# Attention scores of two head groups issued in turns from the lower and the upper 64 partitions, into two PSUM banks

## The chip, the cores and the metric

The kernel runs on one core of a Trainium2 chip. The metric is device time in microseconds (us) of one execution. Three runs of the kernel before took 887.04, 887.59 and 899.56 us (median 887.59). One more execution was profiled; all rows in this text come from it.

## The reference, cut to what matters

Attention over 4 batches, 8 heads, 768 positions and 64 dimensions per head, with a mask (8 global keys and the last 96 local ones) and a bias per head, then two mixture-of-experts layers on its output.

```python
scores = scale * np.matmul(q, k.transpose(0, 1, 3, 2))
scores = scores + bias[None, :, :, :]
scores = np.where(keep, scores, -1000000000.0)
scores = scores - np.max(scores, axis=-1, keepdims=True)
a = np.exp(scores)
a = a / (np.sum(a, axis=-1, keepdims=True) + 1e-09)
attn = np.matmul(a, v)
# x: attn as 3072 rows of 512; then twice, each with 8 experts and the expert of the largest logit:
#   out[row] = gate[row] * (relu(x[row] @ w1[e]) @ w2[e])
```

## The kernel before

**Tiling of the attention.** The 3072 query rows are 24 units of 128 (a batch has six, `QT = 6`). A unit has 8 heads in four groups of two, `HEADS = [(0, 2), (1, 3), (4, 6), (5, 7)]` (L237). Query and key are transposed so that two heads lie one above the other: even heads in partitions 0 to 63, odd heads in 64 to 127. So groups 0 and 2 read the lower half and groups 1 and 3 the upper half (`p0`, L592). A query sees at most 232 keys: 128 of its own block and 104 others (the first unit of a batch: 128 alone).

**The stages of one group g of unit u**, each a function that issues its instructions when called:

- `score` (S, L589): every product is three matmuls (high by high, high by low, low by high part), contracted over 64 partitions. Two heads times two pieces of keys (128 and 104 columns) times three is 12 matmuls, each with a weight load of its own, into one PSUM bank `sp` of the pool tag "A". The first unit of a batch has 6.
- `rowmax` (R, L608), one per head: VectorE (DVE) adds the bias, writes `e` to SBUF and the negative row maximum `nm`. It is the only reader of `sp`; after both, the bank is free.
- `expo` (X, L620): ScalarE (ACT) takes the exponential. `etrans` (T, L625): TensorE (PE) transposes `e`, fp32, four pieces, into a bank `et` of tag "B".
- `e_hi` (EH, L636) on ACT and `e_lo` (EL, L642) on DVE split `et` into a high and a low part, `eh` and `el`.
- `pv` (PV, L648): 12 matmuls with the values, into `xp` of tag "D".

Beside the groups, a unit transposes its keys and queries (`tp`, L555) and its output row (`xtp`, L692), computes the logits (`lp`, L417) and its place in the expert's list (`pr`, L460 to L462), with small work on DVE (L425 to L471, L668 to L702) and splits of query, key and value on GpSimd (POOL).

**What sets the order.** Each tag has two PSUM banks (`bufs=2`, eight banks in all); a third `bank("A", ...)` waits until the first is read out. Nothing is scheduled by a compiler: a `Timeline` sorts all calls by a number, `4 * u + g + OFF[name]`, and calls them in that order (L1095 to L1118); each engine then works strictly in its own order. `OFF` has "S" 0.1, "R0" 0.6, "R1" 0.8, "X0" 1.3, "X1" 1.8, "T0" and "T1" 2.2, "EH" 3.1, "EL" 3.5, "PV" 4.3. So on PE a group's scores stand ahead of the transposes of two groups earlier and of the values' products of four groups earlier, and so on group by group.

**After the attention** the experts' work is one long run of matmuls (L870, L889), whose weights arrive during the attention's last units and are split on ACT and DVE.

Of the kernel before, what the change touches and what calls it, by code (L numbers as in the profile page):

```python
# [12 lines left out]
BF16 = mybir.dt.bfloat16  # L13
# [7 lines left out]
B, H, S, D = 4, 8, 768, 64  # L21
# [23 lines left out]
OFF = {  # L45
# [5 lines left out]
}  # L51
ENG = {
    "kh": "P", "vh": "P", "qh": "P", "mh": "P", "ml": "P", "pp": "P", "pf": "V", "po": "V", "wa": "V",
# [47 lines left out]
def kernel(  # L101
# [3 lines left out]
    nc = tc.nc  # L105
# [20 lines left out]
    def bank(tag, name):  # L126
        return psum.tile([128, 512], F32, tag=tag, name=name)
# [24 lines left out]
    def load(u, nm):  # L152
        b, t = divmod(u, QT)
        q0 = t * 128
        d = st.setdefault(u, {})
        d[nm] = ld.tile([128, H, D], F32, tag=f"ld_{nm}", name=f"ld_{nm}", bufs=4 if nm == "v" else 3)
        nc.sync.dma_start(out=d[nm], in_={"q": q, "k": k, "v": v}[nm][b, :, q0:q0 + 128, :].rearrange("h p d -> p h d"))
# [79 lines left out]
    HEADS = [(0, 2), (1, 3), (4, 6), (5, 7)]  # L237
# [184 lines left out]
    def pick_m(d, lg, row):  # L422

        d["lg"] = lg
        nc.vector.max(out=best_of(row), in_=lg)  # L425

    def pick_i(d, row):
        d["ix"] = small.tile([128, 8], U32, tag="ix", name="ix")
        nc.vector.max_index(out=d["ix"], in_max=best_of(row), in_values=d["lg"])

    def pick_f(d, eng=nc.vector):
        d["ixf"] = small.tile([128, 1], F32, tag="ixf", name="ixf")
        eng.tensor_copy(out=d["ixf"], in_=d["ix"][:, 0:1])

    def pick_o(d, valid, eng=nc.vector):

        oh = d["oh"] = small.tile([128, E], BF16, tag="oh", name="oh")
        if valid is None:
            eng.tensor_scalar(out=oh, in0=iota8, scalar1=d["ixf"], scalar2=None, op0=ALU.is_equal)
        else:  # L440
            nc.vector.tensor_scalar(out=oh, in0=iota8, scalar1=d["ixf"], scalar2=valid, op0=ALU.is_equal, op1=ALU.mult)
# [15 lines left out]
    def place_m(m, d):  # L457

        d["pr"] = bank("C", "pr")[:, 0:E]
        nc.tensor.matmul(out=d["pr"], lhsT=ones_b[0:1, :], rhs=rowoff_b, start=True, stop=False)  # L460
        nc.tensor.matmul(out=d["pr"], lhsT=ones_b, rhs=acc[m], start=False, stop=False)
        nc.tensor.matmul(out=d["pr"], lhsT=before, rhs=d["oh"], start=False, stop=True)  # L462

    def place_t(m, d):
        t2 = small.tile([128, E], F32, tag="t2", name="t2")
        d["pos"] = small.tile([128, 1], F32, tag="pos", name="pos")
        nc.vector.scalar_tensor_tensor(out=t2, in0=d["pr"], scalar=1.0, in1=d["oh"], op0=ALU.mult, op1=ALU.mult,
                                       accum_out=d["pos"])

    def place_a(m, d, eng=nc.vector):  # L470
        eng.tensor_tensor(out=acc[m], in0=acc[m], in1=d["oh"], op=ALU.add)  # L471
# [73 lines left out]
    def t_in(u, nm):  # L545

        d = st[u]
        if nm == "q":
            d["qt"] = aw.tile([128, 2, 4, 128], F16, tag="qt", name="qt", bufs=3)
        else:  # L550
            d["kt"] = kt_of[u] = aw.tile([128, 2, 4, 128 + GMAX], F16, tag="kt", name="kt", bufs=3)
        tp = d["tp", nm] = bank("C", "tp").rearrange("p (i c) -> p i c", i=4)
        src = d[nm].rearrange("p (i e) d -> p i (e d)", e=2)
        for i in range(4):
            nc.tensor.transpose(tp[:, i, :], src[:, i, :], ident)  # L555

    def t_out(u, nm):
        d = st[u]
        f = d["f", nm] = aw.tile([128, 4, 128], F32, tag=f"f{nm}", name=f"f{nm}")
        nc.scalar.activation(out=f, in_=d["tp", nm], func=ACTF.Copy, scale=-0.125 if nm == "q" else 1.0)  # L560
# [27 lines left out]

    def score(u, g):  # L589

        d = st[u]
        p0 = 64 * (HEADS[g][0] % 2)  # L592
        sp = d["sp", g] = bank("A", "sp").rearrange("p (j c) -> p j c", j=2)
        keys = [(slice(WB - 128, WB), d["kt"], 0)]
        if u % QT:
            keys.append((slice(0, NA), kt_of[u - 1], 128 - LMAX + 1))
        else:
            keys[0] = (slice(0, 128), d["kt"], 0)
        for j, h in enumerate(HEADS[g]):
            for cols, kt, c0 in keys:  # L600
                for n, (x, y) in enumerate(((0, 0), (0, 1), (1, 0))):
                    lq = d["qt"][p0:p0 + 64, x, h // 2, :]
                    rk = kt[p0:p0 + 64, y, h // 2, c0:c0 + cols.stop - cols.start]
                    nc.tensor.matmul(out=sp[:, j, cols], lhsT=lq.bitcast(BF16) if x else lq,  # L604
                                     rhs=rk.bitcast(BF16) if y else rk, start=(n == 0), stop=(n == 2),
                                     skip_group_check=True)

    def rowmax(u, g, j):  # L608

# [476 lines left out]
    def off_of(u, nm):  # L1086

        w = (u - NU + 3) / 2 if nm in LAST and u > NU - 3 else 0
        return w * LAST.get(nm, 0) + (1 - w) * OFF[nm]

    def eng_of(nm):
        return nc.gpsimd if ENG[nm] == "P" else nc.vector


    tl = Timeline()  # L1095
    for u in range(NU):
        n = 4 * u
        for nm in "v" if u == 0 else "kqv":
            tl.at(SOFF.get(f"ld{nm}{u}", n + OFF["ld" + nm]), lambda u=u, nm=nm: load(u, nm))
        for nm, fn in (("tq", lambda u: t_in(u, "q")), ("tk", lambda u: t_in(u, "k")),  # L1100
                       ("fq", lambda u: t_out(u, "q")), ("fk", lambda u: t_out(u, "k")),
                       ("qh", q_hi), ("ql", q_lo), ("kh", k_hi), ("kl", k_lo), ("vh", v_hi), ("vl", v_lo),
                       ("rt", route_t), ("rh", route_h), ("rl", route_lo),
                       ("lg", route_l), ("pm", lambda u: pick_m(st[u], st[u]["lp"], st[u]["row"])),
                       ("pi", lambda u: pick_i(st[u], st[u]["row"])), ("pf", lambda u: pick_f(st[u], eng_of("pf"))),
                       ("po", lambda u: pick_o(st[u], None, eng_of("po"))),
                       ("wm", lambda u: place_m(0, st[u])), ("wt", lambda u: place_t(0, st[u])),
                       ("wa", lambda u: place_a(0, st[u], eng_of("wa"))), ("place", route_p)):
            tl.at(SOFF.get(f"{nm}{u}", n + off_of(u, nm)), lambda u=u, fn=fn: fn(u))
        for g in range(4):  # L1110
            for nm, fn in (("S", score), ("EH", e_hi), ("EL", e_lo), ("PV", pv)):
                tl.at(n + g + OFF[nm], lambda u=u, g=g, fn=fn: fn(u, g))
            for nm, fn in (("R", rowmax), ("X", expo), ("T", etrans)):
                for j in range(2):
                    tl.at(n + g + OFF[f"{nm}{j}"], lambda u=u, g=g, j=j, fn=fn: fn(u, g, j))
        for i in range(2):
            for nm, fn in (("fs", fin_s), ("fr", fin_r), ("fx", fin_x)):
                tl.at(n + 2 * i + 1 + off_of(u, nm), lambda u=u, i=i, fn=fn: fn(u, i))  # L1118
# [28 lines left out]
    _, left = slots(tl, 1, t0, t0 + MOFF["table1"])  # L1147
# [30 lines left out]
```

## Time and profile before

| | |
|---|---|
| Three runs | 887.04, 887.59, 899.56 us |
| The profiled execution | 892.53 us (span of its instructions 891.0 us) |
| Attention's scores | from 10.2 to 224.1 us of the span |
| Experts' matmuls end the kernel | the chain that ended last is PE from 634 us on |

The profile names engines PE (matmuls), PEld (weight loads), DVE, ACT, POOL and SP. A busy share is not a measure of what bounds: an engine that is full in a stretch, and has no wait in it, is. Durations of matmuls include their way through the array, so successive matmuls overlap in the list; the pace is read from the starts. "L604" is line 604 of the kernel.

### The profile page before, as it was taken

What the parts mean: (1) busy time and instruction counts of PE and PEld (TensorE: products, weight loads), DVE (VectorE), ACT (ScalarE), POOL (GpSimd) and SP (SyncE); (2) the same over time, 40 slices, a digit from 0 to 9 for tenths busy, and PEclk for the clock granted to TensorE, in tenths of its full rate; (3) what the DMA queues carried; (4) which work ended last, traced back from release to release, by engine and by line L of the source; (5) the groups of instructions that cost most, each with busy time, mean ns of one, the idle gap of its engine ahead of it and who ended that gap; (6) DMA issues with size and microseconds to landing.
All of it is one profiled execution on the core that took longest, in us unless ns stands there. A gap on an engine that the chain in (4) does not pass through costs nothing. (4 is left out here: it accounts for less than half of the span.)

```text
span 891.0 us, 30257 instructions
## 1 busy us (share of the span) xinstructions
PE 830.5 (93%) x10153; PEld 632.3 (71%) x10153; DVE 476.9 (54%) x1745; ACT 401.9 (45%) x858; POOL 305.9 (34%) x495
## 2 busy tenths in 40 slices
PE   5999999999688999999999788969999999999995
PEld 4888888888566777677777566647677777777773
DVE  5668898899843747656573634646311125111133
ACT  5568888888513434525341524332222225222242
POOL 6358777785432333423341422102111111111110
PEclk9999999999699999999999899999999999999998
DMA  8657766677249989987887684832562117322200
GB/s 145 177 150 211 181 147 144 155 193 226 66 104 267 248 185 240 221 262 181 248 240 168 148 216 135 213 116 52 150 162 69 52 50 209 78 62 52 51 28 16
DMA packets 227582, 133.99 MB, mean 150 GB/s; under 512 B 177148, under 2 KB 199676, under 8 KB 227360
## 3 DMA queue, kind: packets, MB, share of 16 engines
q1 hardware_dynamic: 220896, 112.10, 51.5%
q0 software_dynamic: 6320, 19.37, 6.2%
q8 instruction: 85, 1.39, 0.7%
q14 instruction: 137, 1.12, 0.4%
q10 hardware_dynamic: 144, 0.00, 0.0%
HBM read 79.54 MB, written 33.77 MB: 127 GB/s over the span
## 5 line engine op out<-in xcount | busy, mean ns | idle before, releaser
L870 PE MATMUL hp<-mx,h 128*128 128x128 f16 x3520 | 326.4, 222 | 9.6 <-ACTq L896 7.7
L870 PE MATMUL hp<-mx,l 128*128 128x128 f16 x1760 | 312.8, 222 | 7.0 <-DVEq L896 3.9
L870 PEld LDWEIGHTS <-h 128*128 128x128 f16 x3520 | 278.9, 99 | 48.7 <-ACTq L896 10.6
L881 DVE SCALAR_TENSOR_TENSOR hl<-hp,hh 128x256 bf16<-128x256 f32 x220 | 93.1, 423 | 268.7 <-ACT hh L880 139.4
L880 ACT ACTIVATE hh<-hp 128x256 f16<-128x256 f32 x220 | 84.2, 383 | 272.0 <-PE hp L870 233.8
L870 PEld LDWEIGHTS <-l 128*128 128x128 bf16 x1760 | 174.6, 99 | 8.8 <-DVEq L896 4.6
L889 PE MATMUL y<-l,hh 128*128 128x512 bf16 x440 | 167.5, 381 | 1.4 <-DVEq L896 1.4
L889 PE MATMUL y<-h,hh 128*128 128x512 f16 x440 | 167.7, 381 | 0.0
L889 PE MATMUL y<-h,hl 128*128 128x512 f16 x440 | 167.3, 380 | 0.0
L347 DVE TENSOR_TENSOR l<-st,h 128x1024 bf16<-128x1024 f32 x88 | 111.9, 1273 | 52.3 <-ACTq L896 25.3
L889 PEld LDWEIGHTS <-hh 128*128 128x128 f16 x880 | 77.4, 98 | 53.3 <-issue 0.8
L120 ACT CAST h<-st 128x1024 f16<-128x1024 f32 x88 | 91.2, 1043 | 50.7 <-SPq L909 20.7
L934 POOL DMA_INDIRECT out_dram<-o,ti x26 | 27.0, 1040 | 227.3 <-ACTq L896 189.9
L479 POOL DMA_INDIRECT xs<-r,posi x29 | 33.3, 1150 | 176.2 <-DVEq L896 61.3
L623 ACT ACTIVATE e<-e,nm 128x232 f32<-128x232 f32 (+1 forms) x192 | 84.0, 470 | 7.3 <-DVE nm L616 5.1
L889 PEld LDWEIGHTS <-hl 128*128 128x128 bf16 x440 | 43.2, 98 | 54.1 <-issue 2.2
L604 PE MATMUL sp<-kt,qt 64*128 64x128 f16 (+3 forms) x1056 | 77.8, 225 | 2.5 <-DVE nm L616 1.9
L604 PEld LDWEIGHTS <-qt 64*128 64x128 f16 (+1 forms) x1056 | 61.8, 101 | 14.5 <-issue 11.1
L616 DVE CUSTOM_DVE_ANT_0 e<-sp,bias_mid 128x232 f32<-128x232 f32 x160 | 61.3, 385 | 5.7 <-PE sp L604 5.6
L646 DVE TENSOR_TENSOR el<-et,eh 128x512 bf16<-128x512 f32 (+1 forms) x96 | 60.9, 634 | 1.7 <-ACT eh L640 1.7
L640 ACT CAST eh<-et 128x512 f16<-128x512 f32 (+1 forms) x96 | 52.4, 546 | 19.0 <-PE et L634 17.3
L634 PE MATMUL et<-ident,e 128*128 128x128 f32 x192 | 50.7, 297 | 1.0 <-ACT e L623 1.0
(201 smaller groups left out, 1138.9 us busy)
## 6 DMA issues: line engine op xcount, KB each, us to landing
st<-in_moe_w_dram SPq DMA_DIRECT2D x88, 512.0 KB
mxf<-xs SPq DMA_DIRECT2D x29, 266.0 KB
x_d<-r SPq DMA_DIRECT2D x29, 256.0 KB
ld_k<-in_k_dram SPq DMA_DIRECT2D x24, 256.0 KB
ld_q<-in_q_dram SPq DMA_DIRECT2D x24, 256.0 KB
ld_v<-in_v_dram SPq DMA_DIRECT2D x24, 256.0 KB
row<-xg SPq DMA_DIRECT2D x24, 256.0 KB
xs<-empty SPq DMA_DIRECT2D x18, 266.0 KB
```

The lines of the kernel that those rows point to most:

```text
L120: nc.scalar.copy(out=out, in_=in_)
L347: (nc.vector if engines[i][1] == "V" else nc.gpsimd).tensor_tensor(out=l, in0=w, in1=h, op=ALU.subtract)
L604: nc.tensor.matmul(out=sp[:, j, cols], lhsT=lq.bitcast(BF16) if x else lq, rhs=rk.bitcast(BF16) if y else rk, start=(n == 0), stop=(n == 2 ...
L616: nc.vector.tensor_tensor_reduce(out=d["e", g][:, j, 0:w], in0=d["sp", g][:, j, 0:w], in1=(bias_mid if t else bias_first)[:, HEADS[g][j], ...
L623: nc.scalar.activation(out=e, in_=e, func=ACTF.Exp, bias=d["nm", g][:, j:j + 1], scale=-1.0)
L634: nc.tensor.transpose(tp[:, j, :], e[:, j, NA if t else 0:WB if t else 128], ident)
L640: nc.scalar.copy(out=eh[:, 0:n], in_=d["et", g][:, 0:n])
L646: nc.vector.tensor_tensor(out=el[:, 0:n], in0=d["et", g][:, 0:n], in1=d["eh", g][:, 0:n], op=ALU.subtract)
L870: nc.tensor.matmul(out=hp[:, j, :], lhsT=w[p][:, c, fs], rhs=r.bitcast(BF16) if x else r, start=(n == 0), stop=(n == 11))
L880: nc.scalar.activation(out=hh, in_=hp, func=ACTF.Relu)
L881: nc.vector.scalar_tensor_tensor(out=hl, in0=hp, scalar=0.0, in1=hh, op0=ALU.max, op1=ALU.subtract)
L889: nc.tensor.matmul(out=d["y"], lhsT=d[hx, p][:, j, :], rhs=w[p][:, j, :], start=(p == 0 and j == 0 and i == 0), stop=(p == NP - 1 and j == ...
```

## The change

`score` now serves two groups at a time: it takes both banks of tag "A" and issues the matmuls of groups g and g+1 in turns, one from partitions 0 to 63 into the one bank, one from 64 to 127 into the other. Number, shapes and operands of the matmuls and weight loads stay. It is called for even g only, at the even group's number. For the odd group, R is called 0.6 earlier and X 0.3 earlier (`oddR`, `oddX`); T, EH, EL and PV keep their numbers.

```diff
-    "c0s": 1.3, "c1": 15.6, "c1s": 2.0, "rl": 10.6,
+    "c0s": 1.3, "c1": 15.6, "c1s": 2.0, "rl": 10.6, "oddR": 0.6, "oddX": 0.3, "oddT": 0.0,
...
     def score(u, g):
...
-        d = st[u]
-        p0 = 64 * (HEADS[g][0] % 2)
-        sp = d["sp", g] = bank("A", "sp").rearrange("p (j c) -> p j c", j=2)
+        d = st[u]
+        sp = [bank("A", "sp").rearrange("p (j c) -> p j c", j=2) for _ in range(2)]
+        for i in range(2):
+            d["sp", g + i] = sp[i]
...
-        for j, h in enumerate(HEADS[g]):
+        for j in range(2):
             for cols, kt, c0 in keys:
                 for n, (x, y) in enumerate(((0, 0), (0, 1), (1, 0))):
-                    lq = d["qt"][p0:p0 + 64, x, h // 2, :]
...
+                    for i in range(2):
+                        h = HEADS[g + i][j]
+                        p0 = 64 * (h % 2)
+                        lq = d["qt"][p0:p0 + 64, x, h // 2, :]
+                        rk = kt[p0:p0 + 64, y, h // 2, c0:c0 + cols.stop - cols.start]
+                        nc.tensor.matmul(out=sp[i][:, j, cols], lhsT=lq.bitcast(BF16) if x else lq,
+                                         rhs=rk.bitcast(BF16) if y else rk, start=(n == 0), stop=(n == 2),
+                                         skip_group_check=True)
...
         for g in range(4):
-            for nm, fn in (("S", score), ("EH", e_hi), ("EL", e_lo), ("PV", pv)):
+            if g % 2 == 0:
+                tl.at(n + g + OFF["S"], lambda u=u, g=g: score(u, g))
+            for nm, fn in (("EH", e_hi), ("EL", e_lo), ("PV", pv)):
...
             for nm, fn in (("R", rowmax), ("X", expo), ("T", etrans)):
                 for j in range(2):
-                    tl.at(n + g + OFF[f"{nm}{j}"], lambda u=u, g=g, j=j, fn=fn: fn(u, g, j))
+                    t = n + g + OFF[f"{nm}{j}"] - (OFF[f"odd{nm}"] if g % 2 else 0)
+                    tl.at(t, lambda u=u, g=g, j=j, fn=fn: fn(u, g, j))
```

On PE, in a unit in the middle of the attention, the third group's scores start behind the transposes of an output row. Before, the matmuls that follow go to one bank, `sp_3470`:

```order
L692 MATMUL xtp_3460<-ident_97,row_3318 128x128 x4
L604 LDWEIGHTS qt_3121
L604 MATMUL sp_3470<-kt_3039,qt_3121 128x128
L604 LDWEIGHTS qt_3121
L604 MATMUL sp_3470<-kt_3039,qt_3121 128x128
```

In the changed kernel the same place has two banks in turns, `sp_3471` and `sp_3472`, 24 matmuls in all, and the fourth group's place has none:

```order
L697 MATMUL xtp_3460<-ident_97,row_3322 128x128 x4
L609 LDWEIGHTS qt_3122
L609 MATMUL sp_3471<-kt_3053,qt_3122 128x128
L609 LDWEIGHTS qt_3122
L609 MATMUL sp_3472<-kt_3053,qt_3122 128x128
L609 LDWEIGHTS qt_3122
```

So PE has, from one pair's scores to the next, two sets of transposes and two of values' products, where each group's scores stood between them before.

On DVE, in a unit's first two groups, the row maxima (`e,nm<-sp` with `nm` behind it) of one group stood apart from those of the next, with the output's product `row` and a split `el` between them. Before:

```order
L646 TENSOR_TENSOR el<-et,eh 128x512
L616 ISA e,nm<-sp,bias_mid 128x232
L616 ISA nm 128x1
L433 CAST ixf<-ix 128x1
L672 RECIPROCAL rs<-rs 128x4
L616 ISA e,nm<-sp,bias_mid 128x232
L616 ISA nm 128x1
L682 TENSOR_TENSOR row<-xp,rs 128x256
L646 TENSOR_TENSOR el<-et,eh 128x512
L616 ISA e,nm<-sp,bias_mid 128x232
L616 ISA nm 128x1
```

In the changed kernel:

```order
L651 TENSOR_TENSOR el<-et,eh 128x512
L621 ISA e,nm<-sp,bias_mid 128x232
L433 CAST ixf<-ix 128x1
L677 RECIPROCAL rs<-rs 128x4
L621 ISA e,nm<-sp,bias_mid 128x232
...
L621 ISA e,nm<-sp,bias_mid 128x232
...
L621 ISA e,nm<-sp,bias_mid 128x232
L621 ISA nm 128x1
L687 TENSOR_TENSOR row<-xp,rs 128x256
L651 TENSOR_TENSOR el<-et,eh 128x512
```

All four row maxima of the pair now stand together, and `row`, both splits and the small work stand behind the fourth.

## Rows read from the trace of the kernel before

**Rows 1.** The page: span, and its 40 slices of PE, DVE and PEclk.

```profile
span 891.0 us, 30257 instructions
...
PE   5999999999688999999999788969999999999995
...
DVE  5668898899843747656573634646311125111133
...
PEclk9999999999699999999999899999999999999998
```

**Rows 2.** Busy us (and instructions) per engine, seven stretches of one unit each.

```profile
core 0: us, PE busy (x) PEld busy (x) DVE busy (x) ACT busy (x) POOL busy (x), PEclk, DMA share, GB/s
92.88:101.50 8.62, 8.62 (x142) 7.63 (x140) 7.91 (x37) 7.39 (x17) 6.81 (x11) 1.00 0.73 181
...
sum 60.35, PE 60.35 PEld 53.51 DVE 54.66 ACT 51.86 POOL 46.62; mean PE 8.62 PEld 7.64 DVE 7.81 ACT 7.41 POOL 6.66
```

**Rows 3.** PE in order of time, a late unit: start us, us, line, operands, count.

```profile
200.66 0.17 PE L417 MATMUL lp<-wgl,rxh 128*128 128x8 bf16 x1
200.69 0.17 PE L417 MATMUL lp<-wgh,rxl 128*128 128x8 f16 x1
...
211.67 0.19 PE L661 MATMUL xp<-vs,el 128*128 128x65 f16 x1
211.79 0.78 PE L604 MATMUL sp<-kt,qt 64*128 64x128 f16 x12
212.50 0.33 PE L633 MATMUL et<-ident,e 128*128 128x128 f32 x1
...
213.00 0.23 PE L661 MATMUL xp<-va,eh 104*128 104x65 f16 x2
...
213.37 0.63 PE L692 MATMUL xtp<-ident,row 128*128 128x128 f32 x4
213.93 0.78 PE L604 MATMUL sp<-kt,qt 64*128 64x128 f16 x12
```

**Rows 4.** PE in order of time, between 22 and 55 us.

```profile
22.28 1.31 PE L604 MATMUL sp<-kt,qt 64*128 64x128 f16 x12 [1.17 <-DVE nm L616]
...
34.54 1.34 PE L604 MATMUL sp<-kt,qt 64*128 64x128 f16 x12
...
49.32 0.24 PE L661 MATMUL xp<-vs,el 128*128 128x65 f16 x1
49.49 1.34 PE L604 MATMUL sp<-kt,qt 64*128 64x128 f16 x12
50.76 0.47 PE L633 MATMUL et<-ident,e 128*128 128x128 f32 x1
...
54.55 0.33 PE L633 MATMUL et<-ident,e 128*128 128x128 f32 x1
```

**Rows 5.** Busy us per engine, the attention from 54.5 us on and the stretch behind.

```profile
54.50:224.10 169.60, 166.33 (x2639) 145.94 (x2636) 151.72 (x708) 139.63 (x307) 126.14 (x189) 1.00 0.69 178
224.10:245.00 20.90, 12.35 (x164) 10.82 (x162) 18.00 (x50) 12.37 (x20) 9.54 (x13) 0.67 0.21 53
```

**Rows 6.** What PE waited for from 54.5 to 224 us, the largest: us, times, longest.

```profile
PE pr L460 <- DVE rxl L702: 2.3, 4, 0.8
```

**Rows 7.** Groups of instructions, 54.5 to 224 us: busy us, mean ns of one, idle before.

```profile
L623 ACT ACTIVATE e<-e,nm 128x232 f32<-128x232 f32 (+1 forms) x161 | 70.5, 472 | 2.7 <-DVE lead_f L502 1.3 <-DVE nm L616 0.6 <-DVE rs L672 0.5
L604 PE MATMUL sp<-kt,qt 64*128 64x128 f16 (+1 forms) x901 | 60.2, 213 | 0.0
L616 DVE CUSTOM_DVE_ANT_0 e<-sp,bias_mid 128x232 f32<-128x232 f32 x137 | 52.5, 384 | 0.0
L646 DVE TENSOR_TENSOR el<-et,eh 128x512 bf16<-128x512 f32 (+1 forms) x80 | 51.1, 638 | 0.0
L604 PEld LDWEIGHTS <-qt 64*128 64x128 f16 x899 | 47.3, 94 | 8.1 <-issue 6.5
L640 ACT CAST eh<-et 128x512 f16<-128x512 f32 (+1 forms) x81 | 44.5, 550 | 8.8 <-PE et L634 7.2 <-PE xp L661 0.6
```

More of the change, by code (lines that the diff above doesn't have):

```diff
@@ L598, in score @@
             keys[0] = (slice(0, 128), d["kt"], 0)
-        for j, h in enumerate(HEADS[g]):
+        for j in range(2):
             for cols, kt, c0 in keys:
                 for n, (x, y) in enumerate(((0, 0), (0, 1), (1, 0))):
-                    lq = d["qt"][p0:p0 + 64, x, h // 2, :]
[L603 to L606, printed above, removed]
+                    for i in range(2):
[6 more added lines that the diff above has]
+                                         skip_group_check=True)
     def rowmax(u, g, j):
```

## The prediction

> **What bounds the kernel now.** I read the page first: PE is full in nearly every slice, DVE is at 80 to 90% up to the eleventh and well below later [rows 1]. The change touches the attention alone, so it is priced there and carried to the end: behind it PE runs the experts' matmuls almost without a stop, so time won before 224 us should reach the end. Next come the stretches of one unit. They all take 8.62 to 8.63 us; PE fills every one, DVE is busy 7.81 us in the mean, ACT 7.41, POOL 6.66 [rows 2]. From 54.5 to 224.1 us PE is busy 166.33 of 169.60 us [rows 5], and the largest of its few waits, 2.3 us, is for something that the change leaves alone [rows 6]. So in this stretch PE is the bound, with DVE only 0.8 us per unit behind: that 0.8 us, and not what PE saves, is the ceiling of the gain.
>
> Before 54 us it is another regime. The same twelve scores that take 0.71 us from their first start to the next instruction at 211.79 take 1.27 us at 49.49, and the transpose behind them takes 0.47 us in place of 0.33 [rows 3, 4]. TensorE is at the lower of its two levels (1.2 GHz) until some point between 51 and 54.5 us and at 2.4 GHz after, although the page's clock line shows 9 from the first slice [rows 1]; the durations decide. A unit there takes 14.95 us (34.54 to 49.49) [rows 4], far above DVE's 7.8, so PE bounds it with room.
>
> **What a block of scores costs.** At 2.4 GHz: 0.71 us from the first score to the transpose behind it, and ahead of it 0.12 us from the last values' matmul, where such matmuls follow each other at about 0.03 (twelve from 213.00 to 213.37) [rows 3], so 0.09 us of entry. That is 0.80 us, four times a unit, 3.2 of 8.62. The twelve matmuls have (128+104)/2 = 116 columns in the mean, 48 ns at 2.4 GHz, some 0.6 us for twelve; the other 0.2 us is spent on the way in and out of a block.
>
> **The change, part by part.**
>
> *Fewer blocks.* Two blocks of 24 in place of four of 12 save two entries and exits: 2 x 0.2 = about 0.4 us a unit. This part needs no overlap of matmuls.
>
> *Turns between halves.* If a matmul from the lower half runs beside one from the upper half, 24 take the time of 12. No row shows two such matmuls side by side: the halves never met without transposes between them in the stretch read. Bounds: no overlap saves nothing more, PE needs 8.62 - 0.4 = 8.2 us a unit; full overlap makes the pair's block 0.80 us, PE needs 8.62 - 1.6 = 7.0 us. Against overlap stands the issue: every matmul has a weight load. The logits' matmuls, 8 columns each with a weight load of its own, start 25 to 30 ns apart [rows 3], so two loads and two matmuls can be issued in some 52 to 60 ns, about the 48 ns of one stream; issue hardly takes it away. I take full overlap.
>
> The Trainium skill (TensorE: Matmul & The Clock Gate, Measured speedup vs the span model) says that matmuls in different row groups run side by side, each further one costing about 4 ns; by it the pair's block would be 0.85 us by estimate and PE's unit 7.1 us. The same page says that a weight load overlaps a running matmul only when the row groups differ. The trace differs there: loads of 94 ns [rows 7] hide behind matmuls of the same rows, at some 52 ns from one to the next [rows 3], so no gain of that kind is left.
>
> *Who is next.* With PE at 7.0, DVE at 7.81 sets the unit, and ACT at 7.41 is close. PE today reaches 98% of its stretch (166.33 of 169.60) with the runner-up at 90% [rows 5]. DVE would have one runner-up at 95% and stand in a chain with it, so I give it 96%: 7.81 / 0.96 = 8.1 us. Bounds: 7.81 (never idle) and 8.62 (as now).
>
> *The added wait.* A pair needs both "A" banks, so its second matmul waits for the fourth row maximum of the pair before, and transposes and values' products of the older groups queue behind it on PE. The wait's length: four row maxima at 384 ns [rows 7], 1.54 us, and small work between them. PE has 2.3 us of other work behind the scores in the shorter of the two gaps: two sets of transposes at 0.50, two of values' products at 0.37, one row transpose at 0.56 [rows 3]. So PE stands still little there. On the other side DVE has, behind the fourth maximum, two splits of 638 ns [rows 7], 1.28 us, and `row` and small work on top, while the next pair's block takes 0.8 and its last matmul another 0.21 to arrive [rows 7]. DVE stays fed; I cost it at nothing beyond the 96%. If that cover were gone, each pair would cost 1.0 us of DVE, 2.0 a unit. DMA, busy 0.69 of this stretch [rows 5], would rise to 0.74 with the shorter units and stays hidden.
>
> *ACT's new order.* Three exponentials in a row ahead of the odd group's split: 3 x 472 + 550 = 2.0 us [rows 7], then the split on DVE, 0.64, ahead of the next pair's maxima. With the first maximum that is some 3.3 us around, under half a unit at 8.1. No cost.
>
> **Sum.** From 54.5 to 224.1 us: 169.6 x (1 - 8.1/8.62) = 10.2 us. At the bounds: 16 with DVE full; 8 for fewer blocks alone with PE still full; 0 if nothing is won.
>
> From 24.5 to 54.5 us at 1.2 GHz: a block costs 1.27 + 0.11 of entry (49.32 to 49.49 less 0.06, twice the 0.03 above) = 1.38 [rows 4]; two fewer per unit leave 14.95 - 2.76 = 12.2 us. Thirty us hold 2.0 units now and 2.46 then; 0.45 units at the later price of 8.1 are 3.6 us, if the clock rises when it does now. Before 24.5 PE waits for row maxima (1.17 us at 22.28 [rows 4]); I count 0 there, within 1.5 us either way. Behind 224.1 DVE is busy 18.0 of 20.9 us [rows 5] with work that the change leaves alone: 0, up to 2 lost.
>
> Together 13.8 us. The profiled execution took 892.5 us, so its like would take 878.7; it lay 4.9 us over the median of the three runs, 887.6. Against that median: **873.8, say 874 us**.
>
> **The rivals.**
>
> *The clock rises earlier.* PE is dense from 24.5 us on, yet only behind 51 did the clock rise. With half the blocks there are fewer breaks in PE's stream. Every us by which it rises earlier is worth 1 - 8.1/12.2 = 0.34 us; 15 us earlier gives 5 more: 869 us, and 20 us 867. For it: the stream gets denser. Against: nothing in the rows says what made it rise.
>
> *No overlap.* PE needs 8.2 us a unit and stays the bound: 169.6 x 0.4/8.62 = 8 us less at most, and about 0.9 from the slow part (two entries and exits of some 0.2 a unit, two units): 879; with PE held now and then by the two banks, 882.
>
> *The two banks hold PE.* If row maxima come late in each pair, transposes behind the scores come late too, then exponentials' splits, then DVE: a round that closes on itself. At half of the 1.0 us per pair, the unit is 8.1 + 1.0 = 9.1, and 169.6 us become 179: 9.4 - 3.6 = 6 us slower, 893. Against: the cover above, 1.28 us and more against 1.0.
>
> *Slower: the clock stays low.* With DVE the bound, PE stands still a tenth of the time; the clock did fall in the stretch behind the attention (mean 0.67, PE busy 12.35 of 20.9 us [rows 5]). A unit at 1.2 GHz would take 12.2 in place of 8.1, 4.1 us more; from eight units on (a third of the attention) it loses more than 18 us net of the 13.8: 907 and over. Against: where PE now is briefly idle inside the attention, the clock holds.
>
> The Trainium skill (TensorEngine Tiling, PSUM Bottleneck) warns that packing speeds up TensorE but not the reading of PSUM. That is the ceiling above, in rows DVE's 7.81 us; by it the gain is 16 us at most, not the 31 that PE's own saving of 1.6 us a unit would be.
>
> **How the numbers follow.** The forecast, overlap with DVE as the next bound and the clock about as now: 0.45, 865 to 880. Earlier clock: 0.30, 860 to 871. No overlap: 0.10, 877 to 886. Two banks hold PE: 0.08, 883 to 896. Clock stays low: 0.07, over 900. A measurement of this kernel tells about 2%, 18 us, from no change, so faster means under 869.8. The earlier clock gives most of its 0.30 to that (0.26), the forecast 0.10 of its own: faster 0.36, slower (over 905) 0.07, same 0.57. The range that leaves 2 in 10 out: 860 to 889.
>
> **What would show it.** Right: scores of the two banks start in pairs a few ns apart, and 24 take about 0.7 us; PE's share per unit falls to some 85 to 88% with waits named after `nm`, and DVE rises to 95% or more; the unit is 8.0 to 8.3 us. Wrong: 24 matmuls take 1.2 us or more (no overlap); DVE stays at 90% or less with idle time that ends with `sp` (the banks); twelve-score durations above 1 us at a later or earlier time than 54 us (the clock). The stretch behind the scores' end should keep its length; if it grows, DVE's own work was pushed there.

## The result and the profile after

The changed kernel took 865.14 us (median of four, 863.84 to 869.08); the kernel before 890.43 beside it. The ratio is 0.971, with a 95% interval of 0.962 to 0.979. Measured a second time, on another occasion, it took 875.06 us (868.31 to 877.13) against 885.29: 0.989 (0.980 to 0.997). So the change is faster, by 1 to 3%, the second time by less than 2%; the middle of all eight runs is 868.7 us. The range on record (860 to 889) holds both, the sum (874, 13.8 us less) lies between them. The profiled pair that the rest of this text compares, 892.5 and 869.1 us, is of the first measurement.

The page of the changed kernel, the lines that answer [rows 1]:

```profile
span 867.5 us, 30092 instructions
...
PE   4799999895898999999997988979999999999994
...
DVE  4899999998526475647653626465111125111133
...
PEclk9999999997998999999998999989999999999998
```

The span is 23.5 us shorter. DVE is at 80% from the second slice on in place of the fourth, at 90% and more from the third to the ninth, and its full part ends a slice earlier.

Busy time per engine, first of two units that answer [rows 2], then of two stretches of four units, then of the attention from 54.5 us on and what follows (as [rows 5]):

```profile
core 0: us, PE busy (x) PEld busy (x) DVE busy (x) ACT busy (x) POOL busy (x), PEclk, DMA share, GB/s
...
84.42:92.53 8.11, 7.34 (x140) 6.38 (x139) 7.66 (x37) 6.82 (x16) 6.74 (x10) 1.00 0.69 159
92.53:100.51 7.98, 7.24 (x141) 6.39 (x141) 7.72 (x36) 6.85 (x17) 6.52 (x9) 1.00 0.69 165
...
76.22:108.33 32.11, 29.23 (x557) 25.59 (x557) 30.62 (x142) 28.01 (x63) 26.59 (x42) 1.00 0.73 175
122.01:153.05 31.04, 29.02 (x557) 25.49 (x558) 29.99 (x141) 28.32 (x64) 25.90 (x39) 1.00 0.70 162
...
54.50:197.40 142.90, 129.05 (x2401) 111.50 (x2395) 136.90 (x657) 124.29 (x283) 118.99 (x178) 1.00 0.76 195
197.40:218.00 20.60, 11.83 (x151) 10.47 (x149) 17.40 (x47) 10.94 (x17) 10.49 (x12) 0.67 0.25 65
```

Over the eight units of the two stretches a unit takes (32.11 + 31.04) / 8 = 7.89 us in place of 8.62. DVE is busy 96% of it (60.61 of 63.15), PE 92%. In the same eight units before, PE was full and DVE at 89% (61.37 of 69.03):

```profile
91.56:126.11 34.55, 34.55 (x557) 30.63 (x556) 30.73 (x139) 28.68 (x62) 26.47 (x39) 1.00 0.68 161
142.34:176.82 34.48, 34.48 (x557) 30.58 (x556) 30.64 (x139) 29.51 (x63) 26.06 (x39) 1.00 0.62 145
```

The bound has changed hands.

PE in order of time, a pair's block in the middle of the attention and the first blocks, as in [rows 3] and [rows 4]:

```profile
130.06 0.78 PE L609 MATMUL sp<-kt,qt 64*128 64x128 f16 x24
130.77 0.33 PE L638 MATMUL et<-ident,e 128*128 128x128 f32 x1
...
133.22 0.66 PE L697 MATMUL xtp<-ident,row 128*128 128x128 f32 x4 [0.59 <-DMA row<-xg]
133.81 0.79 PE L609 MATMUL sp<-kt,qt 64*128 64x128 f16 x24
```

```profile
20.50 1.34 PE L609 MATMUL sp<-kt,qt 64*128 64x128 f16 x24
...
25.08 0.78 PE L609 MATMUL sp<-kt,qt 64*128 64x128 f16 x23 [0.97 <-DVE nm L621]
...
34.63 0.78 PE L609 MATMUL sp<-kt,qt 64*128 64x128 f16 x24
```

24 scores take the 0.71 us that 12 took. And the block at 25.08 already runs at 2.4 GHz, where the kernel before still ran at 1.2 GHz at 50 us.

**Where the time went**, from the starts of scores in the two profiles:

| part | before | after | difference |
|---|---|---|---|
| first score to the fifth unit's first score | 48.4 us | 36.0 us | -12.4 |
| from there to the last score | 165.4 | 150.7 | -14.7 |
| last score to the first expert's matmul | 14.8 | 17.3 | +2.5 |
| from there to the end | 652.1 | 653.2 | +1.1 |

The middle line is the shorter unit. The first line is the clock above all: in a later profile of the kernel before, whose clock was high from 29 us on, that part took 36.9 us, next to the 36.0 here (and the middle part 162.5). In the third line DVE is busy 15.22 of the 17.3 us, in place of 13.64 of 14.8, so 1.6 of the 2.5 us are more work of DVE in that part. In the last part the clock was low for longer: once for 6.8 us (granted clock 0.50 from 262 us on, against 3.4 us from 286.5 on before), and in one stretch of 3.4 us more. That this makes the 1.1 us is likely and not shown.

### The profile page after: what moved, and what is told of

The parts are those of the page before. It is cut to its first block, busy times and chain, and to the rows that moved or that the text cites. A ratio compares the mean times of both kernels' runs of the same rounds, so it can differ in the third digit from the quotient of the medians.

```text
span 867.5 us, 30092 instructions
## 1 busy us (share of the span) xinstructions
PE 782.7 (90%) x10045; PEld 592.5 (68%) x10153; DVE 470.9 (54%) x1745; ACT 397.0 (46%) x858; POOL 303.9 (35%) x495
## 5 line engine op out<-in xcount | busy, mean ns | idle before, releaser
L894 PE MATMUL y<-l,hh 128*128 128x512 bf16 x332 | 127.7, 385 | 1.4 <-DVEq L901 1.4
L628 ACT ACTIVATE e<-e,nm 128x232 f32<-128x232 f32 (+1 forms) x192 | 80.9, 468 | 4.3 <-DVE nm L621 3.1
L621 DVE CUSTOM_DVE_ANT_0 e<-sp,bias_mid 128x232 f32<-128x232 f32 x160 | 58.9, 382 | 0.3 <-PE sp L609 0.2
L639 PE MATMUL et<-ident,e 128*128 128x128 f32 x192 | 47.6, 283 | 3.0 <-ACT e L628 2.6
L638 PE MATMUL et<-ident,e 128*128 128x128 f32 x160 | 42.9, 295 | 1.8 <-DVE rs L673 1.2
L666 PEld LDWEIGHTS <-eh 104*128 104x128 f16 (+1 forms) x704 | 43.2, 100 | 1.9 <-ACT h L120 0.7
```

What stands on the lines that cost most here:

```text
L621: nc.vector.tensor_tensor_reduce(out=d["e", g][:, j, 0:w], in0=d["sp", g][:, j, 0:w], in1=(bias_mid if t else bias_first)[:, HEADS[g][j], ...
L628: nc.scalar.activation(out=e, in_=e, func=ACTF.Exp, bias=d["nm", g][:, j:j + 1], scale=-1.0)
L639: nc.tensor.transpose(tp[:, j, :], e[:, j, NA if t else 0:WB if t else 128], ident)
L666: nc.tensor.matmul(out=xp[:, h % 4, 0:w], lhsT=l, rhs=r, start=(n == 0), stop=(n == len(ops) - 1), skip_group_check=True)
L894: nc.tensor.matmul(out=d["y"], lhsT=d[hx, p][:, j, :], rhs=w[p][:, j, :], start=(p == 0 and j == 0 and i == 0), stop=(p == NP - 1 and j == ...
```

## The experiments

"Unit" is the mean of the same eight units wherever it is given, two stretches of four. Ratios are to runs of the kernel before beside them (medians 885.3 to 886.0 us).

**Is it the overlap? The groups one after the other.**

```diff
-        for j in range(2):
-            for cols, kt, c0 in keys:
-                for n, (x, y) in enumerate(((0, 0), (0, 1), (1, 0))):
-                    for i in range(2):
+        for i in range(2):
+            for j in range(2):
+                for cols, kt, c0 in keys:
+                    for n, (x, y) in enumerate(((0, 0), (0, 1), (1, 0))):
```

> The changed kernel with everything in its place (24 scores in one block, both banks, the same order of row maxima and exponentials), but the matmuls of the two groups one after the other, 12 from the lower half, then 12 from the upper. If the overlap of the two halves is what shortens the unit: a block of 24 takes about 1.33 us in place of 0.71, PE needs 7.05 + 1.24 = 8.3 us a unit and is the bound again, the unit is 8.3 to 8.5 us in place of 7.85, some 20 units give +9 to +13 us: 874 to 878. If fewer blocks and the new order did it: 865, unit 7.9. If the clock's earlier rise hangs on the overlap too, it rises behind 40 us again and the time is above 880.

Measured 872.16 us (868.65 to 880.04), ratio 0.984 (0.980 to 0.988); unit 8.21 us. The block takes 1.15 us, not 1.33: where the twelfth lower matmul meets the first upper ones, several still run side by side. So it is a weak version of the change, and the next one is the clean control of the overlap.

**Both groups from the lower half.** Same turns, same two banks, same order of calls; the odd heads' scores are computed from the even heads' data.

```diff
-                        p0 = 64 * (h % 2)
+                        p0 = 0
```

> The changed kernel with both groups of a pair read from the lower 64 partitions: the same instructions in the same turns into the same two banks, but the odd heads' scores are computed from the even heads' data. If it is the two halves of the array that let matmuls run side by side: a block of 24 takes 1.15 us again (as with the groups one after the other), the unit 7.87 or more, about 870 to 878. If the turns between two banks did it, 0.71 us and 865 to 870.

Measured 877.9 us (one run); unit 8.58 us. PE in order of time, and the first of its stretches of four units:

```profile
128.64 1.39 PE L609 MATMUL sp<-kt,qt 64*128 64x128 f16 x24
129.96 0.33 PE L638 MATMUL et<-ident,e 128*128 128x128 f32 x1
```

```profile
78.03:112.72 34.69, 33.58 (x557) 30.17 (x557) 30.46 (x141) 27.86 (x63) 26.35 (x39) 1.00 0.69 162
```

24 scores take 1.32 us (128.64 to 129.96), more than the 1.15 I had put down, and PE is busy 97%. So it is the two halves that make matmuls run side by side; the two banks and the turns alone do not. Without the overlap the unit is 8.58 us against 8.62. Yet fewer blocks did shorten PE's stream. Where PE has no wait, a unit takes 8.26 us, as in the first line below, or 8.24, the next one. In the other six of the eight units PE waits for the DMA of the output row, the second line (from 78 to 162.6 us: us, times, longest), and that takes the gain back:

```profile
146.08:154.34 8.26, 8.26 (x140) 7.52 (x140) 7.45 (x36) 6.74 (x17) 6.51 (x10) 1.00 0.68 157
PE xtp L697 <- DMA row<-xg: 3.0, 7, 1.3
```

Its clock rose at 29 us all the same.

**Is DVE the next bound? More and less of DVE.** First one split per unit done twice; then three small steps moved to POOL, in the changed kernel and in the one before.

```diff
-        nc.vector.tensor_tensor(out=el[:, 0:n], in0=d["et", g][:, 0:n], in1=d["eh", g][:, 0:n], op=ALU.subtract)
+        for _ in range(2 if g == 0 else 1):
+            nc.vector.tensor_tensor(out=el[:, 0:n], in0=d["et", g][:, 0:n], in1=d["eh", g][:, 0:n], op=ALU.subtract)
```

> The changed kernel with the low part of each unit's first group (el on DVE, about 0.63 us) computed twice, the same values to the same place: 0.63 us more of DVE a unit (0.33 in a batch's first). If DVE bounds the unit now (7.54 of 7.85 busy): the unit goes to 8.4 us, some 22 x 0.6 = 12 to 14 us more than the changed kernel, about 880 to 884 on this chip, where its close relatives took 870. If the hand-overs or PE bound it, DVE's 0.3 us of idle time and PE's wait take part of it: 4 to 7 us more, 874 to 877.

```diff
-    "kh": "P", ..., "pp": "P", "pf": "V", "po": "V", "wa": "V",
+    "kh": "P", ..., "pp": "P", "pf": "P", "po": "P", "wa": "P",
```

> The changed kernel with three small steps of each unit's placing (the index's cast, the one-hot, the running sum: 150, 372 and 292 ns on DVE) on POOL. DVE then needs 6.8 us a unit, PE 7.0, ACT 7.0. If DVE alone bounds: the unit goes to 7.2 to 7.4, 9 to 12 us less, about 858 to 861. If the chain through ACT and PE is as tight as DVE: 7.7, 0 to 4 us less, 866 to 870. If POOL's steps come late for the place: no gain, 870 or more.

> The kernel before with the same three small steps moved from DVE to POOL that saved the changed kernel about 0.3 us a unit. Before, PE is full in a unit of 8.62 us: if PE bounds it, the unit stays 8.62 at the high clock and the time lies among the runs of before, 877 to 899. If DVE was as tight as PE: units of 8.3, -6 us.

Measured: 883.14 us (878.85 to 885.21; ratio 0.998, 0.994 to 1.002) with more DVE, 860.57 us (859.77 to 867.35; ratio 0.977, 0.967 to 0.987) with less, and 889.17 us (one run) for the kernel before with less. The first stretch of four units of each, in this order:

```profile
79.07:114.27 35.20, 29.55 (x559) 25.61 (x558) 34.85 (x147) 28.00 (x62) 26.31 (x39) 1.00 0.65 156
```

```profile
73.78:104.50 30.72, 28.72 (x557) 25.32 (x558) 29.03 (x131) 27.91 (x63) 29.12 (x54) 1.00 0.75 181
```

```profile
91.54:126.02 34.48, 34.48 (x557) 30.57 (x557) 28.58 (x124) 29.09 (x62) 29.56 (x52) 1.00 0.69 162
```

With more DVE the unit is 8.72 us, DVE full (34.85 of 35.20). That is 0.83 us more for an added split of 0.68, and over the 8.4 I expected: the one-hot (`oh`, L439) took longer too, 910 ns in the mean of the eight units against 337. With less it is 7.59 us, DVE at 95%. In the kernel before, 0.5 us less of DVE a unit (28.58 against some 30.7 in four units) leaves the unit at 8.62, PE full. So DVE bounds the changed kernel and did not bound the one before. The step from 7.89 to 7.59 is 0.30 us, less than I expected (7.2 to 7.4): DVE's busy time fell by 0.38 us a unit, where I had counted on 0.7. POOL and ACT are at 95% and 92% there; that the chain through them holds the rest was not tried. By its median it is the fastest kernel of this study, though its slowest run lies among those of the changed kernel.

The one-hot makes DVE's busy time vary. In the kernel before and in the changed one, every one-hot of more than 300 ns (17 and 16 of 53) ends 23 to 33 ns behind the end of the POOL instruction that was running when it began. So by these rows it waits for POOL, and the wait counts as busy; why it has to, no run here shows. One of them, before:

```profile
137.68 1.16 POOL L568 TENSOR_TENSOR qt<-fq,qt 128x512 bf16<-128x512 f32 x1
137.72 1.15 DVE L439 TENSOR_SCALAR oh<-iota,ixf 128x8 bf16<-128x8 f32 x1
```

**PE's new wait.** The transposes of the output row were called behind the pair's scores.

```diff
-"rt": 10.0,
+"rt": 10.15,
```

> The changed kernel with the transposes of the output row called behind the second pair's scores (number 10.15 in place of 10.0), so that their wait for the row's DMA, 14 us in all in front of those scores, no longer holds the scores. If DVE bounds the unit (7.54 of 7.85 us busy), PE's wait was free: 863 to 867, unit 7.8. If PE's wait counts: 0.3 to 0.6 us a unit less, 853 to 860.

Measured 871.53 us (868.64 to 873.19), ratio 0.984 (0.980 to 0.987); unit 7.90. No gain: PE's waits for the row's DMA, 14.2 us in all in the changed kernel, were free there, where DVE bounds. PE's longest wait from 54.5 us on is for row maxima instead:

```profile
PE sp L609 <- DVE nm L621: 6.0, 15, 0.7
```

**The order of the odd group.**

```diff
-"oddR": 0.6, "oddX": 0.3, "oddT": 0.0,
+"oddR": 0.0, "oddX": 0.0, "oddT": 0.0,
```

> The changed kernel without the earlier calls of the odd group's row maxima and exponentials (0.6 and 0.3 put to 0). The fourth row maximum then stands behind the output's product and a split, about 1.1 us later, and only one split is left behind it as cover for the next pair's scores (1.0 us). If this order is part of the gain: DVE idles 0.2 to 0.5 us a pair, the unit is 8.2 to 8.7, 872 to 882. If the overlap alone does it: 865 to 870, unit 7.85.

Measured 871.11 us (869.93 to 873.69), ratio 0.986 (0.979 to 0.992), next to 875.06 for the changed kernel in the same comparison. The unit is 8.13 us against 7.89 and 7.98, 0.15 to 0.24 longer, under what I expected, and not by idle time of DVE, as I had it: DVE is busy 97% (62.85 of 65.07 us), and its one-hot takes 673 ns in place of 337. In whole times the clock's play hides the difference.

**The clock.** Matmuls of constants in PE's idle time at the start, in both kernels.

```diff
+    def warm_pe(k):
+        ps = bank("D", "hotp")
+        for _ in range(k):
+            nc.tensor.matmul(out=ps, lhsT=hot[:, 0:128], rhs=hot, start=True, stop=True)
+
+    warm_pe(14)
...
+        if u == 0:
+            warm_pe(4)
```

> The kernel before with matmuls of constants added: 14 while PE waits for the first loads, 4 behind each of the first unit's four score blocks; their results are not read. If the clock rises by 10 us in place of 54 and stays: the 30 us from 24.5 to 54.5 hold 2.0 units at 14.95 us, which take 17.2 us at 8.62, so 12 to 13 us less: 876 to 878, with the late units unchanged at 8.62. If the low clock there was not the price (PE would wait for others anyway): 888 to 892.

> The changed kernel with the same added matmuls (14 at the start, 8 behind each of the first unit's two score blocks, where PE waits 2.6 us each time). Its clock rises at 23 us by itself, and before that PE waits for row maxima most of the time: if so, -2 to 0 us, 863 to 866. If the low clock before 23 us matters: -5 us or more, 860.

Measured 882.65 us for the first (878.14 to 898.79; ratio 0.997, 0.992 to 1.002) and 869.84 for the second (868.56 to 872.22; ratio 0.982, 0.979 to 0.985), against 885.62 for the kernel before. The first missed: the clock did rise at 5 us, but in its one profile (the slowest of its ten runs, 898.79 us) it fell again at 22 us for 17 us, and at 175.5 us for 41 us. So the early rise did not last there. The second did not gain either, as expected, though its time lies above the 863 to 866 that I gave. The experiment decides nothing on the price.

So the kernel before was profiled twice more.

> The kernel before, unchanged, profiled once more. Its runs so far spread from 877.5 to 899.6 us. If the spread is the time at which TensorE's clock rises (and whether it falls again in the attention): with the first profile's 14.95 us a unit at the low level and 8.62 at the high one, every us of dense attention at the low level costs 0.42 us, so the time should be 891 plus 0.42 times the change of the low level's length against the first profile's 30 us, within 3 us. If the spread has another source, the clock rises near 54 us again whatever the time.

> The same once more: the first profile's relation (0.42 us for every us of the attention at the low level) should hold for a third length, or the rise stands at 54 us again and the theory of the clock falls.

The second profile took 877.24 us, the third 887.01. PE in order of time in the second:

```profile
27.56 1.34 PE L604 MATMUL sp<-kt,qt 64*128 64x128 f16 x12
30.07 0.78 PE L604 MATMUL sp<-kt,qt 64*128 64x128 f16 x12
```

and in the third, with a stretch later on:

```profile
34.01 1.34 PE L604 MATMUL sp<-kt,qt 64*128 64x128 f16 x12
37.88 0.92 PE L604 MATMUL sp<-kt,qt 64*128 64x128 f16 x12
40.17 0.78 PE L604 MATMUL sp<-kt,qt 64*128 64x128 f16 x12
```

```profile
160.00:174.80 14.80, 13.91 (x219) 11.88 (x217) 13.34 (x61) 11.38 (x26) 11.55 (x19) 1.00 0.71 156
174.80:195.20 20.40, 20.40 (x178) 17.53 (x179) 12.13 (x59) 10.32 (x23) 12.93 (x22) 0.50 0.69 168
```

The clock rose at 29 us in the second (after 3.4 us at the high level from 18.6 us on), at 38 us in the third, and in the third it fell once more for 20 us, in which PE was full. From 24.5 us on that makes 4, 34 and (first profile) 30 us of the attention at the low level. By 0.42 us each I expected 880 and 893 us. The 891 I started from is the first profile's span, so the spans compare: 875.8 and 885.5, the one 4, the other 7 us below, both outside my 3 us. In the attention itself the price is right: the two units of the third profile that fell into its 20.4 us took 13.05 and 11.94 us where the same two units of the second profile took 7.83 and 8.63, 8.5 us more, or 0.42 for each us. The rest is that units at a batch's start were shorter than in the first profile (7.1 and 7.4 against 7.8 to 8.3), and stretches behind the attention that also differ by a few us.

Last, the changed kernel again.

> The changed kernel, unchanged, on this chip beside the kernel before. Theory: 10 to 12 us of its gain are the shorter unit (against the second profile of before, 877.2 us, whose clock was high from 28.8 us on), the rest is that its clock rises early and does not stay low again. Then its runs should lie within some 6 us of each other, 863 to 870, where those of before spread over 20, and the profile should show no low stretch of over 7 us between 25 and 195 us. If its first four runs were only lucky with the clock, single runs above 875 turn up.

Measured 875.06 us (868.31 to 877.13), ratio 0.989 (0.980 to 0.997): runs within 9 us of each other, not 6, two of them above 875, so the first four were also lucky. Unit 7.98. Its clock was low for 3.4 us twice between 25 and 195 us, as expected.

## Why the prediction was right or wrong

**The total: right, in part by luck.** The middle of the eight runs, 868.7 us, is 5 us under the sum. But one part of the sum, the clock's, was off by 8.8 us in the profiled pair, and how much the change is worth in whole times hangs on where the clock rises in the kernel before, which varies from run to run. On record a gain too small to tell had 0.57 and a clear one (under 869.8 us) 0.36; the two medians, 865.14 and 875.06, lie on either side of that line.

**Overlap: right.** 24 scores in 0.71 us, full overlap. PE's need, 7.0 in the forecast, is 7.0 us by the starts in the unit from 133.81 to 141.25 us: 7.44, in which PE's stream stands still for 0.43 ahead of the row's transposes. By busy time, which counts the last matmuls' way through the array ahead of each wait, it is more, 58.24 / 8 = 7.28. The issue of weight loads did not hold it up.

**Fewer blocks: right for PE.** I priced it at 0.4 us a unit; with one half alone PE needs 8.25 us where it has no wait, so it is 0.37. (By busy time, 66.87 / 8 = 8.36, it looks like less, since each wait counts a last matmul's way through the array as busy.) The saving of 1.6 us is thus 0.37 from fewer blocks and 1.2 from the overlap, as in the sum. What the forecast for a change without overlap lacked is the wait for the row's DMA: there the unit stayed at 8.58.

**The next bound: right, share for share.** DVE at 96% was the guess and is measured (94.5% in the second profile). Its own need was mis-sized: 7.81 us a unit carried from [rows 2], 60.61 / 8 = 7.58 us after. More than half of that is the choice of units: the same eight units took 61.37 / 8 = 7.67 us of DVE before. Of single instructions, the one-hot took 408 ns in the mean of these units before and 337 after; the splits did not change (678 and 677 ns for those of 128x512). In the two later profiles of the kernel before, the same eight units took 7.92 us of DVE, so such differences lie within what one kernel shows. So 8.1 became 7.89 to 7.98, just under the 8.0 to 8.3 named as the sign, and the unit's term, from the fifth unit on, 14.7 us in place of 10.2 in the profiled pair. Of these 14.7, 2.9 belong to the first profile, whose units at a batch's start were longer: against the second profile of the kernel before the term is 11.8.

**The added wait: right.** From 23 us to the last score PE waited 2.5 us in all for row maxima ahead of scores, in three places:

```profile
PE xtp L697 <- DMA row<-xg: 14.2, 20, 2.4
PE sp L609 <- DVE nm L621: 2.5, 3, 1.0
PE tp L555 <- DVE t L467: 0.5, 2, 0.3
```

The wait that is there, for the row's DMA, I had not named; it costs nothing, since DVE is the bound. So two signs on record did not show: PE's waits are not named after `nm` in the main, and PE is busy 92% of a unit, not 85 to 88%.

**The clock: the likeliest case was wrong, its rival happened.** The forecast let the clock rise as before and gave 3.6 us for the slow part; the rival, an earlier rise, had 0.30. It rose 31 us earlier (23.1 against 54.4), which at the rival's 0.34 us is 10.6 us on top. Measured is 12.4 us for the first four units against 3.6, 8.8 on top. That, and 4.5 us of the unit's term, less 3.6 given back behind, make the step from 13.8 to 23.5 us.

The step that failed is deeper than the choice: I took the first profile's clock for the kernel's. Its rise in the kernel before is not a fixed place: 54, 29, 38 and (with the three small steps moved) 58 us in four profiles, and in one of them it fell again for 20 us. Against the second profile, with the clock high from 29 us on, the change is worth 12.6 us up to the last score and 8.3 us at the end. In all nine profiles of kernels with blocks of 24, the one without overlap too, the clock was high from 41 us on at the latest, and fell again before the last score for 6.8 us at most. That the longer blocks do this is not shown: one of the four profiles before rose as early, at 29 us, and stayed high up to the last score. What makes the clock rise stays open; the overlap is not needed for it, since it rose at 29 us with one half alone (one profile).

**The warning on PSUM** in the Trainium skill (TensorEngine Tiling, PSUM Bottleneck) is borne out: by overlap PE's need fell by 1.2 us a unit (8.25 to 7.0), the unit by 0.6 to 0.7 (8.58 to 7.89 and 7.98), and DVE, which reads PSUM, is left at 96%. DVE's time is not the reading alone, though: three small steps that touch no PSUM were worth 0.3 us of the unit.

**Behind the attention** I allowed up to 2 us lost; it was 2.5 up to the first expert's matmul and 1.1 after, 3.6 together, more than allowed.

## What to carry to other kernels

Contractions over 64 partitions ran two at a time when they alternated between the halves and wrote different banks (one bank for both was not tried), and the gain is capped by whoever reads the banks: price the reader first. Busy time hides waits: PE's counted the way through the array, DVE's one-hot the wait for POOL; read the need of an engine from the starts in a stretch without waits. Before a stretch at the low clock goes into a sum, profile the same kernel more than once; where the clock rises at a different time in each run, one profile's rise can be worth as much as the change. And once a bound has moved, work that was free on the new one (three small steps on DVE here) is worth moving.

## What the runs showed of the hardware

Two scores from different halves run at once. In stretches of 20 and 10 ns, a block's start in the changed kernel has two matmuls running, then four, as the first pair is still on its way through the array when the second starts:

```profile
133.80:133.82 0.02, 0.01 (x2) 0.02 (x3) 1.00 0.00 0
133.87:133.88 0.01, 0.01 (x4) 0.01 (x6) 1.00 0.00 0
```

and in the kernel before one, then two:

```profile
142.34:142.36 0.02, 0.02 (x1) 0.02 (x2) 1.00 0.07 0
142.41:142.42 0.01, 0.01 (x2) 0.01 (x3) 1.00 0.06 0
```

The Trainium skill (TensorE: Matmul & The Clock Gate, Measured speedup vs the span model) gives about 4 ns for the second matmul of a pair; the trace's starts, taken from one matmul to the next in the block at 133.81, are 3 to 4 ns apart within a pair and 42 to 63 ns from pair to pair.

A full PE did not by itself bring the clock back: in the third profile of the kernel before, PE was busy 20.40 of 20.40 us at a granted clock of 0.50, and in the first it ran without a gap at 1.2 GHz from 24.5 to 54.4 us. I had not expected that a stream without a gap could stay at 1.2 GHz so long.
